# Linear attention with a gated feed-forward layer on one core: a written-out order for all engines, the query decay moved into a cast, even and odd tokens sorted by the store, scores and state alternating, and inter-block products at full size

## The chip, the cores and the metric

One Trainium2 chip, one of its cores. The time is device microseconds of a whole execution, the median of several runs. A profile is one execution seen by the hardware profiler; its span is 1 to 2 us shorter than the time. Engines are named as in the profile: PE is the tensor engine, PEld its weight loads, DVE the vector engine, ACT the scalar engine, POOL GpSimd, SP the engine that issues the transfers (SPq is its queue). Two views are used most. The slices cut the span into 40 equal parts; a digit is the busy share of a part in tenths (9 is 90% or more). The chain of work that ended last starts at the last instruction and goes back, at each step, to whatever released it; a line gives start, length, engine, tile and line of the kernel. GB/s is what all DMA engines together moved.

The profile lists PE's products as 128*128 ("full array") or 64*64 ("64 rows", four quadrants); going from one kind to the other is called a change of its tiling mode here (0.109 us each in the runs below). An eviction is a copy of PE's result out of PSUM. FFN is the feed-forward layer. The turns are products with the identity that bring the result back to rows of tokens.

A ratio of two kernels is the mean time of the fast runs of one over the mean time of the fast runs of the other in the same rounds on the same chip, with a 95% interval. It is therefore not quite the ratio of the medians that are quoted.

## The reference, cut to what matters

```python
# q, k, v: [4, 8, 768, 64]; lam: one decay per head; blocks of 64 tokens
for b in range(nb):
    intra = (qb @ kb.T * Dmask) @ vb               # Dmask[i, j] = lam ** (i - j) for i >= j
    inter = (qb * lam_pow) @ kv_state
    out[b] = intra + inter
    kv_state = lam_block * kv_state + (kb * rev_pow).T @ vb
x = out, tokens x 512                              # 3072 x 512
H = max(x @ w_h, 0);  T = sigmoid(x @ w_t + b_t)
result = T * H + (1 - T) * x
```

Both kernels write the decay as a product: v is scaled by lam^-t and the queries' side by lam^t, so the mask is only a triangle of ones and zeros and the state needs no decay of its own. A step of both is 256 tokens (twelve steps). A partition holds two neighbouring tokens of k, q and v (`(p j)` with j = 0, 1), so a load reads 512 contiguous bytes at a time. After a transpose the 128 tokens of a half stand as "all even ones, then all odd ones". Somewhere they must come back into order; where this happens is one part of the change.

## The kernel before: what the change and the argument touch

The kernel records tasks and a small planner in Python (a model of engine times) sorts them into one static order.

```python
def evac_q(n, p, hs, eng):                   # here even and odd tokens come back into order
    dst = get("qT", n)[:, hs.start // 2:hs.stop // 2].rearrange("p n (q j) -> p n q j", j=J)
    src = get("qtr", n, p).rearrange("p n j q -> p n q j")
    A.activation(dst, src, AF.Copy) if eng == "ACT" else V.tensor_copy(dst, src)

def inter(n):                                # 64-row products, one per head
    ...
    T.matmul(get("o", n)[half(e), b, hp, :], lhsT=get("ss", n, b)[half(e), hp, :],
             rhs=get("qT", n)[half(e), hp, b * C:(b + 1) * C], ...)

def decay(n, b):                             # lam^t, after the attention, on DVE
    V.tensor_tensor(get("xT", g)[:, :, r * C:(r + 1) * C], in0=get("o", n)[:, b],
                    in1=pow_q[:, :, c * C:(c + 1) * C], op=ALU.mult)

def store(n, b, p, js):
    i = (2 * n + b) * C
    nc.sync.dma_start(out=out[i:i + C, js[0] * 128:js[-1] * 128 + 128], in_=get("o_sb", n, b, p))

for t in plan(tasks):
    t.emit()
```

## Time and profile before

| | before |
|---|---|
| time, median of 3 runs | 119.21 us (119.08 to 121.41) |
| span of the profile | 118.0 us, clock granted 1.0 throughout |
| busy: PE, DVE, ACT, POOL | 98.8, 81.1, 70.7, 52.3 us |
| moved by DMA | 27.3 MB, of which 6.29 MB are stores |

The prediction below reads the slices and the chain of waits. One further view of the kernel before is needed for the end of the story: the issues of the store line on the SP queue. The columns of the first line are the number of issues, the time of one issue on SP in ns (minimum, median, maximum) and the first and last start.

```profile
L397 SPq DMA_DIRECT2D out_dram<-o_sb x25: 332/407/1930, 37.3 to 115.2; - x25
...
DMA to landing us min/median/max: 1.9/4.8/6.4
```

A store of 256 KB holds SP for about 0.4 us and has landed 4.8 us later. In the profile no engine waits for one, except at the very end of the program (1.4 us).

### The profile page before, as it was taken

How to read it: one execution, taken by the hardware profiler on the slowest of the kernel's cores; microseconds unless marked ns; L12 is line 12 of the kernel's file. 1: busy time of each engine (PE TensorE's matmuls, PEld its weight loads, DVE VectorE, ACT ScalarE, POOL GpSimd, SP SyncE). 2: the span in 40 equal slices, each digit the busy share in tenths (PEclk: the TensorE clock that was granted, in tenths of full speed). 3: DMA queues.
4: the chain of work that ended last, by engine and by line, in shares of the span. 5: the costliest groups of instructions: out<-in, count | busy, mean ns of one | idle time of the engine just before them, and what ended most of it. 6: DMA issues, size and time to landing. Idle time of an engine off the chain costs nothing.

```text
span 118.0 us, 4685 instructions
## 1 busy us (share of the span) xinstructions
PE 98.8 (84%) x2049; PEld 83.0 (70%) x2049; DVE 81.1 (69%) x138; ACT 70.7 (60%) x135; POOL 52.3 (44%) x52
## 2 busy tenths in 40 slices
PE   0056548776899999999999999999988999999970
PEld 0044436565688878888888888888777888888950
DVE  0539461229768887969869788698698775988460
ACT  3599203393874665784677757837576578353860
POOL 7148432777585765864484647458360000000000
PEclk9999999999999999999999999999999999999999
DMA  0999999899999999999999999999912204004045
GB/s 17 267 304 380 366 294 284 234 252 305 289 293 272 301 290 290 305 300 322 335 290 315 304 265 300 300 315 263 314 64 89 94 0 173 10 6 178 6 178 177
DMA packets 42413, 27.57 MB, mean 234 GB/s; under 512 B 1301, under 2 KB 38425, under 8 KB 42393
## 3 DMA queue, kind: packets, MB, share of 16 engines
q1 hardware_dynamic: 42240, 27.27, 82.4%
q8 instruction: 16, 0.26, 1.0%
q14 instruction: 5, 0.03, 0.1%
q10 hardware_dynamic: 152, 0.01, 0.1%
HBM read 20.98 MB, written 6.29 MB: 231 GB/s over the span
## 4 chain that ended last, share of the span: by engine, by line
PE 67%; DMA 12%; DVE 7%; SPq 4%; issue 3%; ACT 2%; POOL 1%; DVEq 0%
PE w L367 33%; PE w L385 9%; DMA qf<-in_q_dram 8%; PE w L299 8%; PE s L317 6%; PE o L341 5%; DMA w_f<-in_moe_w_h_dram 4%; DVE th L379 4%; SPq L282 4%; PE kv L349 3%; PE o L330 3%; DVE m L321 2%; ACT L376 1%; POOL qb L286 1%; ACT t_sb L376 1%
## 5 line engine op out<-in xcount | busy, mean ns | idle before, releaser
L367 PE MATMUL w<-xT,w_b 128*128 128x256 bf16 (+1 forms) x416 | 49.0, 268 | 0.0
L367 PEld LDWEIGHTS <-w_b 128*128 128x128 bf16 x416 | 36.9, 99 | 4.6
L321 DVE TENSOR_TENSOR m<-s,tri 128x512 bf16<-128x512 f32 x48 | 31.6, 684 | 4.0 <-PE s L317 3.5
L376 ACT ACTIVATE t_sb<-w,bt_col 128x256 bf16<-128x256 f32 (+1 forms) x52 | 21.0, 458 | 18.6 <-PE w L367 17.1
L292 POOL TENSOR_TENSOR vs<-vf,pow_k 128x1024 bf16<-128x1024 f32 (+1 forms) x13 | 23.1, 1778 | 11.7 <-DMA vf<-in_v_dram 9.1
L355 DVE TENSOR_TENSOR xT<-o,pow_q 128x512 bf16<-128x512 f32 x24 | 15.4, 685 | 11.4 <-PE o L341 11.4
L371 DVE SCALAR_TENSOR_TENSOR hmx<-w,xT 128x512 bf16<-128x512 f32 (+1 forms) x26 | 16.7, 642 | 5.5 <-PE w L367 5.4
L286 POOL CAST qb<-qf 128x1024 bf16<-128x1024 f32 (+1 forms) x13 | 12.7, 979 | 16.4 <-DMA qf<-in_q_dram 13.9
L379 DVE TENSOR_TENSOR th<-t_sb,hmx 128x512 bf16<-128x512 bf16 (+1 forms) x26 | 15.8, 606 | 4.7 <-ACT t_sb L376 4.5
L391 ACT ACTIVATE o_sb<-w 128x512 f32<-128x512 f32 (+1 forms) x24 | 13.7, 588 | 7.3 <-PE w L385 7.3
L303 ACT ACTIVATE kT<-w 128x1024 bf16<-128x1024 bf16 (+1 forms) x13 | 12.4, 954 | 6.5 <-PE w L299 6.5
L308 ACT ACTIVATE qT<-w 128x1024 bf16<-128x1024 bf16 x11 | 11.3, 1024 | 7.4 <-PE w L299 7.4
L286 POOL CAST kb<-kf 128x1024 bf16<-128x1024 f32 x11 | 11.9, 1079 | 5.3 <-DMA kf<-in_k_dram 5.3
L385 PE MATMUL w<-id,th 128*128 128x128 bf16 x96 | 13.1, 219 | 0.6 <-DVE th L379 0.6
L385 PE MATMUL w<-id,xT 128*128 128x128 bf16 x96 | 13.2, 220 | 0.0
L317 PE MATMUL s<-qT,kT 64*64 64x128 bf16 x384 | 11.5, 229 | 1.5 <-DVE m L321 1.4
L349 PE MATMUL kv<-vs,kb 64*64 64x64 bf16 x320 | 9.2, 198 | 2.1 <-POOL vs L292 1.4
L349 PEld LDWEIGHTS <-kb 64*64 64x64 bf16 x320 | 7.6, 113 | 4.2 <-issue 4.2
L299 PE MATMUL w<-id,kb 128*128 128x128 bf16 x96 | 8.4, 235 | 2.5 <-POOL kb L286 1.9
L317 PEld LDWEIGHTS <-kT 64*64 64x64 bf16 x384 | 7.5, 110 | 3.9 <-DVE m L321 2.4
L385 PEld LDWEIGHTS <-th 128*128 128x128 bf16 x96 | 9.3, 98 | 1.1 <-DVE th L379 1.0
L385 PEld LDWEIGHTS <-xT 128*128 128x128 bf16 x96 | 9.1, 98 | 1.0
(37 smaller groups left out, 78.3 us busy)
## 6 DMA issues: line engine op xcount, KB each, us to landing
out_dram<-o_sb SPq DMA_DIRECT2D x23, 256.0 KB, 4.8
kf<-in_k_dram SPq DMA_DIRECT2D x11, 512.0 KB, 7.3
qf<-in_q_dram SPq DMA_DIRECT2D x11, 512.0 KB, 7.8
vf<-in_v_dram SPq DMA_DIRECT2D x11, 512.0 KB, 7.1
w_f<-in_moe_w_h_dram SPq DMA_DIRECT2D x4, 256.0 KB, 5.2
w_f<-in_moe_w_t_dram SPq DMA_DIRECT2D x4, 256.0 KB, 5.6
kf<-in_k_dram SPq DMA_DIRECT2D x2, 256.0 KB, 4.7
qf<-in_q_dram SPq DMA_DIRECT2D x2, 256.0 KB, 5.5
```

The costliest lines, as they stand in the source:

```text
L286: eng.tensor_copy(get(x + "b", n)[:, :, hs, :].rearrange("p j h d -> p h j d"), get(x + "f", n, p).rearrange("p h (j d) -> p h j d", j=J))
L292: eng.tensor_tensor(get("vs", n)[:, hs].rearrange("p h j d -> p (h j) d"), in0=get("vf", n, p).rearrange("p h (j d) -> p (h j) d", j=J), i ...
L299: T.transpose(get(x + "tr", n, p)[:, i, j, :], get(x + "b", n)[:, j, h:h + 2, :], id128)
L317: T.matmul(get("s", n, u)[half(b), e, i, j, :], lhsT=get("kT", n)[half(e), hp, j, half(b)], rhs=get("qT", n)[half(e), hp, b * C:(b + 1) * ...
L321: V.tensor_tensor(get("m", n, u)[:, e], in0=get("s", n, u)[:, e], in1=tri[:, None].to_broadcast([128, 2, J, C]), op=ALU.mult)
L349: T.matmul(get("kv", n // NST)[half(e), hp, :], lhsT=get("kb", n)[half(b), j, 2 * hp + e, :], rhs=get("vs", n)[half(b), 2 * hp + e, j, :], ...
L355: V.tensor_tensor(get("xT", g)[:, :, r * C:(r + 1) * C], in0=get("o", n)[:, b], in1=pow_q[:, :, c * C:(c + 1) * C], op=ALU.mult)
L367: T.matmul(get(x, g, js[0])[:, i, :], lhsT=w[:, kc, j * 128:(j + 1) * 128], rhs=get("xT", g)[:, kc, :], start=(kc == 0), stop=(kc == KC - 1))
L371: V.scalar_tensor_tensor(get("hmx", g, js[0]), in0=get("h", g, js[0]), scalar=0.0, in1=get("xT", g)[:, js[0]:js[-1] + 1, :], op0=ALU.max, ...
L376: A.activation(get("t_sb", g, js[0])[:, i, :], get("t", g, js[0])[:, i, :], AF.Sigmoid, bias=bt_col[:, j:j + 1])
L379: V.tensor_tensor(get("th", g)[:, js[0]:js[-1] + 1, :], in0=get("t_sb", g, js[0]), in1=get("hmx", g, js[0]), op=ALU.mult)
L385: T.matmul(get("x", n, b, p)[:, (j - js[0]) * 128:(j - js[0] + 1) * 128], lhsT=get(x, g)[:, j, r * C:(r + 1) * C], rhs=id128, start=(j == ...
```

## The change

Its intent: take the planner's order out and write down one order for all engines, found elsewhere, with a better start; take work off the vector engine; and make tensor-engine work cheaper by fewer changes of its tiling mode. The core of the diff (the order itself, some forty lines of tokens such as `TQ.0.0=0`, is cut):

```diff
-class Task: ...
-def plan(tasks): ...
+PLAN = """
+Lq.0.0 Lq.0.1 Lq.1.0 Lk.0.1 Lv.0.1 Lk.0.0 Lv.0.0 Lk.1.0 CQ.0.1@POOL Lq.1.1 Lv.1.1 ...
+"""
 # query decay: in the cast of q on POOL, no longer after the attention
-    eng.tensor_copy(get(x + "b", n)..., get(x + "f", n, p)...)
+def cast_q(n, p, eng):
+    scale(n, p, eng, "qf", new(("qb", n), ...)..., pow_q)
-    V.tensor_tensor(get("xT", g)..., in0=get("o", n)[:, b], in1=pow_q[...], op=ALU.mult)
+    copy(eng, new(("xT", *g), ...)[:, :, r * C:(r + 1) * C], get("o", n, b))       # DVE or ACT
 # even and odd tokens: no longer sorted at the eviction of q, but by the store
-    dst = get("qT", n)[...].rearrange("p n (q j) -> p n q j", j=J)
-    src = get("qtr", n, p).rearrange("p n j q -> p n q j")
+    copy(eng, new(("qT", n), [128, NP, J, C])[...], get("qtr", n, p))
-    nc.sync.dma_start(out=out[i:i + C, ...], in_=get("o_sb", n, b, p))
+    nc.sync.dma_start(out=out[i:i + C, cs].rearrange("(q j) d -> j q d", j=J), in_=get("o_sb", n, b, p))
 # scores and state alternate
+    for i, (hp, j, x) in enumerate(...):
+        score(n, e, hp, j, x)
+        if st:
+            state(n, b, *st[i])
 # inter: the state is kept as a 128 x 128 block diagonal, one full product for two heads
-    T.matmul(get("o", n)[half(e), b, hp, :], lhsT=get("ss", n, b)[half(e), hp, :], rhs=get("qT", n)[half(e), ...], ...)
+    T.matmul(get("o", n, b)[:, hp, :], lhsT=get("ss", n, b)[:, hp, :], rhs=get("qT", n)[:, hp, :, half(b)], ...)
 # the sigmoid stays in PSUM; its table is loaded ahead
+    A.preload_act_table(AF.Sigmoid)
```

## The prediction

> **What bounds the kernel now.** I read the slices of the page first, because they show whether one limit holds for the whole span.
>
> ```profile
> PE   0056548776899999999999999999988999999970
> PEclk9999999999999999999999999999999999999999
> DMA  0999999899999999999999999999912204004045
> ```
>
> A digit is a slice of 2.95 us. TensorE (PE) is filled from slice 11 (about 33 us) to slice 38, and only partly before that; the DMA engines are full from 3 to 88 us. So there are three stages: a start, in which TensorE waits, a middle, in which it does not, and a tail. The chain of work that ended last, in order of time, names what holds each. First the start:
>
> ```profile
> 6.13 5.03 DMA w_f<-in_moe_w_h_dram
> 11.18 9.08 DMA qf<-in_q_dram
> 20.31 1.05 POOL qb L286
> 21.41 1.05 PE w L299 x8
> 23.52 1.28 ACT L376
> 25.68 1.29 DVE th L379
> 26.98 1.21 DVE m L321 x2
> 28.23 0.42 PE s L317 x16
> ```
>
> Until 20 us the chain is loads: both weight matrices (2 MB) are fetched ahead of the second block's k, q and v, and the second q lands at 20.26. Then come one-time costs in a row: a table load on ScalarE (ACT), a product on VectorE (DVE), two masks. One whole period of the middle, in the same view:
>
> ```profile
> 67.54 0.57 PE o L341 x32
> 68.11 0.30 PE kv L349 x16
> 68.41 1.85 PE w L367 x16
> ...
> 70.86 0.45 PE o L330 x15
> 71.30 0.55 PE w L299 x8
> 71.85 0.87 PE w L367 x8
> 72.73 0.45 PE w L385 x8
> 73.17 0.35 PE s L317 x16
> 73.52 0.55 PE w L385 x8
> 74.07 0.45 PE w L299 x8
> 74.52 0.87 PE w L367 x8
> 75.39 0.57 PE o L341 x32
> ```
>
> No link belongs to another engine: the pieces add up to the period, 75.39 - 67.54 = 7.85 us for a block of 256 tokens. Periods without a second state update take 7.55. Twelve blocks (8 x 7.85 + 4 x 7.55) are 93 us of TensorE issue time. From 33 us to its last matmul at 114.4 TensorE loses about 2.5 us (waits near 39.7, 86.3 and 113.2 to 114.0), so 79 us of the work lie there and 14 before 33 us: **19 us are lost in the start, 2.5 in the middle, 3.6 in the tail** (114.4 to 118.0: last eviction and store).
>
> [...]
> - [...]eight transposes take 0.45 us after other full-array work and 0.55 after 64-row work (67.54 period), and sixteen scores 0.42 against 0.35.
> - [...]the mask, 512 elements from PSUM, takes 684 ns; the gate product on bf16 in SBUF has a median of 415. No contiguous bf16 copy from PSUM on VectorE is in it.
> - [...]The gate product's longest, 1.72 us against the median of 415 ns[...].
> [...]
>
> **The change part by part.** The instruction orders of both builds give the counts.
>
> **Order of the start.** Before, the weights are loads 7 to 14 of the queue. Now fifteen half loads (256 KB) of blocks 0 to 2 come ahead, and the weights follow in four transfers of 512 KB spread between loads of blocks 2 and 3. In the trace before, 256 KB land every 0.75 us from 5.6 us (first k) to 15.4 (last weights), and every 0.86 later. Applied to the new order: blocks 0 and 1 complete at about 13.9 us (before: 22.0), the first half of w_h at 17.9, the second at 20.5, those of w_t at 24 and 26.5, block 3 at about 31. The casts on POOL then pace the start. The decay in the q cast makes it a product like v's, 1.91 us against 1.05 a block. POOL does q0, half of k0 and v0 from about 6.7 us, q1, k1, v1 by 16.5, q2 by 18.4, and v3 at about 33. What TensorE can finish by 33 us is therefore: attention of blocks 0 to 2 (transposes 3.0, scores and state 3.5, inter and intra 2.9), the FFN of blocks 0 and 1 (eight groups of eight matmuls at 0.9: 7.2), one such group of block 2 (0.9), block 3's transposes (1.0), the four turns of blocks 0 and 1 (2.0): 20 us, against 14. **Gain: about 5.5 us.** The sigmoid table is also loaded ahead of time (1.28 us off the chain above), which is inside this figure.
>
> **Inter as full products.** 160 matmuls of 64 rows (0.45 us a block) become 80 of 128x128; at the 0.055 us of a transpose or turn, eight take 0.45. No gain by itself, but inter leaves the 64-row mode. With the new grouping the mode changes fall from 68 to 42 in the built orders. At 0.07 to 0.10 us each, 26 fewer are **2.2 us**. The state eviction doubles in width, 382 to about 597 ns (as the output eviction of 512), 20 times.
>
> **Scores and state alternating.** Sixteen scores take 0.35 and sixteen states 0.24 to 0.30 apart; together 0.59 where they touch. Thirty-two intra products in all four quadrants take 0.57. Alternated scores and states keep four quadrants busy too, so I expect 0.57 a pair. [...] Sum: 0 (within 1 us).
>
> **Query decay in the POOL cast.** The decay product on VectorE (24 x 685 ns) becomes a plain copy of the same length, which ScalarE can take: 13 do. POOL rises by 13 x some 0.85 = 10 us, to about 62; its 4.9 us a block lie under the 7.6 of TensorE after the start.
>
> **Even-odd to the store.** The permuted q eviction becomes contiguous. The relu product takes 682 ns for 512 elements and 424 for 256, so 1.01 ns an element and 0.165 us fixed[...]. ScalarE stays at 1.02. The store's rows keep their length. The sigmoid now stays in PSUM, so the gate product costs 684 ns flat: its mean was 663 with the long ones. Nothing.
>
> **VectorE and ScalarE.** VectorE: masks 32.8, relu 16.7, gate 16.7, eleven copies of o 7.5, ten states 6.8, kT and qT 7.2, the rest 5: 93 us of durations (before 81). Back to back two take 1.28, not 1.37, so some 87 in effect. ScalarE about 71, as before.
>
> **Tail.** Behind the last blocks stand 12 turn matmuls that don't need the last gate; before, TensorE waited 0.9 us there. I take 0.5 us, as a 256 KB store now precedes the last one closely.
>
> **Sum.** TensorE: 93 - 2.2 = 91 us of work; 20 done at 33 us, 71 left, 2 us of waits: last matmul at 106. Tail 3.5: span 109.5. The time is 1.2 us above the span (119.21 against 118.0): **110.7 us**.
>
> **The rivals.**
> 1. *VectorE becomes the bound.* 69 of its 91 us follow after 33 us, against 71 of TensorE: for it speaks that a fixed order leaves it almost no room, against it that overlap makes 69 into 65. Waits of 3 to 5 us: 114 to 116 us.
> 2. *POOL or the loads hold the start.* Every cast is one block late if the DMA is irregular, as it was before (the second k at 17.1, the second q only at 20.3, where 0.86 a load would give 18.4). For it: v3 on POOL at 33 us is just in time. Then the start gives 2 us, not 5.5: 114 us.
> 3. *The start is hidden better than I count, or alternation lets scores hide states* (0.45 a pair: 2 us less on TensorE): 107 to 108 us.
> 4. *Only the order of the start matters and TensorE's work is unchanged*, if the mode change costs nothing: 113 us.
>
> **Range and chances.** Rivals 1 and 2 each have perhaps one chance in four and cost 3 to 5 us, rival 3 one in four and gives 3. So 107.5 to 115.0 us. Faster by over 2% (below 116.8) needs only half of the start's gain: 0.93. Within 2%: 0.05. Slower: 0.02; it would take a wait in every block.
>
> **What would show it.** The PE row of the slices should be filled from slice 8 to 10 on; the second v's cast on POOL should end by 17 us; the first FFN matmul should start near 19 us. In the middle the chain should still be TensorE alone, with a mean period near 7.4 us a block, full-array groups of eight at 0.45 more often than 0.55, alternated pairs near 0.57, eight inter products 0.45. VectorE near 93 us busy, POOL near 62, ScalarE near 71. I am wrong if VectorE links fill the chain after 33 us (rival 1), if "DMA" or POOL ends TensorE's waits up to 40 us (rival 2), or if a period is longer than 7.7 us.

## The result, and the profile after

| | before | after |
|---|---|---|
| time, median of 4 runs | 119.14 us (118.24 to 121.41) | **197.79 us** (197.68 to 198.47) |
| ratio | | 1.665 (1.655 to 1.675) |
| span of the profile | 118.0 us | 196.0 us, mean clock 0.79 |
| busy: PE, DVE, ACT, POOL | 98.8, 81.1, 70.7, 52.3 us | 102.5, 84.3, 64.8, 60.9 us |

The result is correct, and it is slower by two thirds. The prediction was 110.7 us with a range up to 115. No compute engine is busy for over 9 us more than before; yet 78 us of span have been added. The slices of the changed kernel (one digit is 4.9 us) show where, with the bandwidth of the DMA engines in the last row:

```profile
PE   0268999999999060696097096999800000000000
...
PEclk9999999999999855599669859999985555555555
DMA  4999999999663147933455211111111111111110
GB/s 118 297 290 317 322 302 282 294 294 285 198 188 97 52 146 206 264 128 111 142 161 172 96 53 54 55 51 54 51 51 51 52 51 51 51 51 51 50 51 33
```

Three things are to be seen. PE is filled from slice 4 to slice 12 (20 to 64 us, counted from 0), earlier than before, as predicted. Then it has holes; the DMA row has thinned out before that, from slice 10 on (49 us). And from slice 29 on nothing computes; the DMA engines go on at 51 GB/s with a busy share of one tenth, where they moved about 300 GB/s at nine tenths. Stretches of the same profile (length, busy time of PE, PEld, DVE, ACT, POOL with the number of instructions, granted clock, DMA share, GB/s):

```profile
33.00:56.00 23.00, 23.00 (x531) 20.38 (x528) 20.65 (x34) 15.41 (x27) 18.18 (x12) 1.00 0.99 265
56.00:70.00 14.00, 7.46 (x130) 6.33 (x132) 8.07 (x14) 4.53 (x10) 4.79 (x3) 0.89 0.35 109
70.00:102.00 32.00, 18.54 (x296) 15.75 (x292) 11.58 (x19) 9.76 (x16) 9.59 (x6) 0.68 0.54 164
...
142.00:196.00 54.00, 0.00 (x0) 0.00 (x0) 0.00 (x0) 0.00 (x0) 0.00 (x0) 0.53 0.13 49
```

From 33 to 56 us PE is busy without a gap (23.00 of 23.00). The first store is issued at 47 us; the transfers thin out from 49 us on, and PE runs dry at about 64 us. In the last 54 us only stores move: 49 GB/s at a share of 0.13 of 16 engines. **0.13 is about 2/16: as if two of the sixteen DMA engines carried the stores, at about 25 GB/s each.** No view names a single engine, so this is a reading that the experiments have to test. The clock is lower (0.68, 0.53) in the stretches in which PE is partly or wholly idle; in the last 54 us nothing computes, so there it costs nothing. The issues of the store line, in the columns explained above:

```profile
L337 SPq DMA_DIRECT2D out_dram<-o x23: 625/3602/7202, 47.2 to 176.4; - x23
```

The SP queue of the same profile in order of time (start, length, what):

```profile
58.39 4.81 SPq L337 DMA_DIRECT2D out_dram<-o  x2
63.30 4.45 SPq L173 DMA_DIRECT2D qf<-in_q_dram  x1
...
110.56 60.66 SPq L337 DMA_DIRECT2D out_dram<-o  x13
```

An issue of a store now takes 3.6 us in the median, not 0.4, and the issue of the load queued behind two of them takes 4.45. The chain of work that ended last (start, length) says the same: the tensor engine waits for a cast of q, the cast for a load, and the load lands 8.9 us after its issue (qb is the cast q, qf and kf the loads).

```profile
56.94 8.88 DMA qf<-in_q_dram
...
66.05 1.90 POOL qb L191
...
102.26 8.93 DMA kf<-in_k_dram
```

The built programs tell what differs in the store. The listing of the SP instructions (not a profile) has 128 contiguous rows before and a pattern with 2 in front after:

```
before:  L397 DMACopy out_dram<-o_sb    128x512
after:   L337 DMACopy out_0_dram<-o     2x64x512
```

### The profile page after: what moved, and what is told of

It is laid out like the page before. It is cut to its first block, busy times and chain, and to the rows that moved or that the text cites. A ratio compares the mean times of both kernels' runs of the same rounds, so it can differ in the third digit from the quotient of the medians.

```text
span 196.0 us, 4558 instructions
## 1 busy us (share of the span) xinstructions
PE 102.5 (52%) x1969; PEld 88.5 (45%) x1969; DVE 84.3 (43%) x144; ACT 64.8 (33%) x120; POOL 60.9 (31%) x51
## 3 DMA queue, kind: packets, MB, share of 16 engines
HBM read 20.98 MB, written 6.29 MB: 139 GB/s over the span
## 4 chain that ended last, share of the span: by engine, by line
SPq 26%; PE 23%; DMA 13%; issue 5%; POOL 3%; DVE 1%; ACT 1%; POOLq 0%; DVEq 0%; ACTq 0%
SPq L173 21%; PE bt L300 7%; PE bh L300 5%; DMA kf<-in_k_dram 5%; DMA qf<-in_q_dram 5%; DMA w_f<-in_moe_w_t_dram 4%; PE bx L327 3%; SPq L337 3%; PE bs L217 2%; SPq L178 2%; POOL vs L191 2%; PE bo L282 2%; PE bo L272 1%; PE bqtr L205 1%; POOL qb L191 1%
## 5 line engine op out<-in xcount | busy, mean ns | idle before, releaser
L256 DVE TENSOR_TENSOR m<-bs,tri 128x512 bf16<-128x512 f32 x48 | 31.1, 681 | 6.1 <-PE bs L217 5.8
L300 PE MATMUL bh<-xT,w_b 128*128 128x256 bf16 (+1 forms) x208 | 27.6, 284 | 0.3 <-DVE w_b L105 0.2
L191 POOL TENSOR_TENSOR qb<-qf,pow_q 128x1024 bf16<-128x1024 f32 (+1 forms) x13 | 22.9, 1769 | 15.1 <-DMA qf<-in_q_dram 11.4
L191 POOL TENSOR_TENSOR vs<-vf,pow_v 128x1024 bf16<-128x1024 f32 (+1 forms) x12 | 21.9, 1833 | 12.8 <-DMA vf<-in_v_dram 12.8
L300 PE MATMUL bt<-xT,w_b 128*128 128x256 bf16 (+1 forms) x208 | 24.9, 270 | 0.4 <-POOL w_b L105 0.4
L305 DVE SCALAR_TENSOR_TENSOR hm<-bh,xT 128x512 bf16<-128x512 f32 (+1 forms) x26 | 16.3, 642 | 20.3 <-PE bh L300 20.3
L314 ACT ACTIVATE bt<-bt,bt_col 128x256 f32<-128x256 f32 (+1 forms) x52 | 21.9, 431 | 8.9 <-PE bt L300 7.9
L318 DVE TENSOR_TENSOR th<-bt,hm 128x512 bf16<-128x512 f32 (+1 forms) x26 | 16.6, 644 | 2.9 <-ACT bt L314 2.2
L217 PE MATMUL bs<-qT,kT 64*64 64x128 bf16 x384 | 16.0, 233 | 0.3 <-DVE qT L105 0.3
L327 PE MATMUL bx<-id,th 128*128 128x128 bf16 x96 | 14.1, 231 | 0.3 <-DVE th L318 0.3
```

The lines of the kernel that those rows point to most:

```text
L191: ENG[eng].tensor_tensor(dst, in0=get(src, n)[:, heads(p)].rearrange("p h (j d) -> p h j d", j=J), in1=pw[:, n % NST, heads(p), :, None].t ...
L217: T.matmul(get("s", n, e, hp // 2)[half(b), hp % 2, j, :], lhsT=get("kT", n)[half(e), hp, j, half(b)], rhs=get("qT", n)[half(e), hp, :, ha ...
L256: V.tensor_tensor(new(("m", n, e, u), [128, 2, J, C]), in0=get("s", n, e, u), in1=tri[:, None].to_broadcast([128, 2, J, C]), op=ALU.mult)
L300: T.matmul(t[:, r, :], lhsT=w_b[w][:, kc, (2 * u + r) * 128:(2 * u + r + 1) * 128], rhs=get("xT", *g)[:, kc, :], start=(kc == 0), stop=(kc ...
L305: V.scalar_tensor_tensor(new(("hm", g, u), [128, 2, z * C], tag=f"hm{z}"), in0=get("h", g, u), scalar=0.0, in1=get("xT", *g)[:, 2 * u:2 * ...
L314: A.activation(dst[:, r, :], src[:, r, :], AF.Sigmoid, bias=bt_col[:, 2 * u + r:2 * u + r + 1])
```

## The experiments

The theory after this reading, **leading dimension**: a transfer is spread over the DMA engines by its outermost dimension; with 2 there, two engines carry it. Loads would be spread over all 16, so that a load is complete only when its sixteenths on those two engines are through, behind the stores; this last part is argued, as no view follows one load over the engines. So far the theory rests on the share of 0.13 of 16 engines alone.

Rivals: **stride** (rows 4 KB apart in memory are slow to write) and **order of the queue** (the written-out order puts stores between loads, which holds the loads back).

### Two stores in place of one

```diff
-        nc.sync.dma_start(out=out[i:i + C, cs].rearrange("(q j) d -> j q d", j=J), in_=get("o_sb", n, b, p))
+        for j in range(J):
+            nc.sync.dma_start(out=out[i:i + C, cs].rearrange("(q j) d -> j q d", j=J)[j], in_=get("o_sb", n, b, p)[half(j)])
```

> The changed kernel, but each store is issued as two, one for the even and one for the odd rows (64 rows of 2 KB each, same rows at the same places, result right). Theory 'leading dimension': the 2 x 64 x 512 form of the store is carried by 2 of the 16 DMA engines (51 GB/s and a DMA share of 0.13 in its last 54 us); with 64 rows in front all 16 work, the tail of 54 us and the load waits between 56 and 120 us go, and the time is near the 110.7 us predicted (107 to 115). Rival 'stride': rows 4 KB apart in memory are what is slow; then it stays above 180 us. Rival 'order of the queue': stores between loads in the SyncE queue hold the loads back; then the waits from 56 to 120 us stay and the time is above 135 us.

Measured: 118.61 us, ratio to before 0.9935 (0.986 to 1.001), correct. (The experiments were run in several calls; each ratio is against runs of the kernel before in the same rounds, so ratios of different calls can be compared, and medians only roughly.) The same rows go to the same places, 4 KB apart, in the same order of the queue, and 79 us are gone. That removes stride and order of the queue as causes of the loss. It is not the 107 to 115 us that the theory expected, though; the missing microseconds (6.4 against the next run) are followed up below.

### The plain store, rows in wrong order

```diff
-        nc.sync.dma_start(out=out[i:i + C, cs].rearrange("(q j) d -> j q d", j=J), in_=get("o_sb", n, b, p))
+        nc.sync.dma_start(out=out[i:i + C, cs], in_=get("o_sb", n, b, p))
```

> The changed kernel with the plain contiguous store of before (128 rows in order; the even and odd tokens land in wrong rows on purpose). Leading dimension: like the run with two stores, 107 to 115 us, perhaps 1 us less for half the number of stores. Stride: also fast, so this run alone does not tell the two apart. Order of the queue: above 135 us.

Measured: 112.18 us, ratio 0.9403 (0.934 to 0.947); wrong. Everything else in the change is as it was, so everything else together gains 6%. It also lies within the range that was predicted for the whole.

### The kernel before, with only the form of its store changed

```diff
-        nc.sync.dma_start(out=out[i:i + C, ...], in_=get("o_sb", n, b, p))
+        nc.sync.dma_start(out=out[i:i + C, ...].rearrange("(q j) d -> j q d", j=2), in_=get("o_sb", n, b, p))
```

> The kernel before, with only its store written in the 2 x 64 x 512 form (rows wrong on purpose). Leading dimension: stores at 51 GB/s carried by 2 engines, which also carry 2/16 of 21 MB of loads: 6.29 + 2.62 MB at 51 GB/s = 174 us of their time, so 180 to 205 us, with a DMA share of 0.13 at the end. Order of the queue (a fault of the written-out order): stays near 119 us.

> The kernel before with its store in a 4 x 32 x 512 form (rows wrong on purpose, rows 8 KB apart). Leading dimension: 4 engines, 102 GB/s and a share of 0.25 where stores run alone; 6.29 + 5.24 MB at 102 GB/s = 113 us of their time, so 120 to 135 us. Stride: at least as slow as the 2 x 64 form, 180 us or more.

Measured (rows wrong): 199.27 us with 2 in front, ratio 1.673 (1.659 to 1.687), and 144.5 us with 4 in front (two runs, 142.25 and 146.78, the profiled one slow, so no ratio is given). The slices' last rows, first with 2, then with 4:

```profile
DMA  4999999944754442754472472441111111111110
GB/s 103 311 377 293 256 281 292 263 127 140 197 156 142 151 138 61 223 137 147 142 207 71 144 200 79 147 139 48 55 55 51 55 51 51 51 51 51 51 50 33
```

```profile
DMA  1999999999976776666776577667652222222220
GB/s 45 295 348 375 293 265 281 286 285 277 273 217 200 196 196 212 181 179 208 206 200 180 162 208 211 184 200 210 198 148 96 101 94 98 85 101 88 100 94 27
```

Where only stores are left, 2 in front moves about 51 GB/s, 4 in front 85 to 101 GB/s: nearly twice as much with twice the dimension, at about twice the share (0.13 from 144 to 198 us; 0.27 from 107 to 137 us). The kernel before has another order, another decay and other products, and one line brings it to the time of the changed kernel. So the store alone is enough, and the theory agrees with these runs. The time with 4 was expected at 120 to 135 us and came out longer; my sum took the engines' data time only and no waits.

### The rows in order again, twice

If the sorting is not the store's business, it can be done where the attention result is copied out of PSUM (a copy of fp32: on DVE 683 ns for 512 elements, as long as a contiguous bf16 copy takes for 1024, 680 ns), or, as before, at the eviction of q.

```diff
 def take(n, b, eng):
-    copy(eng, new(("xT", *g), ...)[:, :, r * C:(r + 1) * C], get("o", n, b))
+    copy(eng, new(("xT", *g), ...)[:, :, r * C:(r + 1) * C].rearrange("p n (q j) -> p n q j", j=J),
+         get("o", n, b).rearrange("p n (j q) -> p n q j", j=J))
```

> The changed kernel, with the even and odd tokens put back into order where the attention result is copied out of PSUM (one copy per 128 tokens, same number of elements), and the plain contiguous store. Result right. Theory: the order of the rows costs nothing there[...]; so it is the 112.2 us of the run with the plain store in wrong order (111 to 113.5), 0.94 of the kernel before. Rival: a stepped read of PSUM is slow; then the 24 copies take over 750 ns (now about 600 to 684) and the time is above 114 us.

Measured: **112.05 us, ratio 0.9356 (0.929 to 0.943), correct.** The copies take 683 ns on DVE and 595 on ACT, as the contiguous ones of the run with the plain store do (683 and 595). Three of its six runs are slow; the three fast ones average 111.4 us, and the ratio uses these alone.

The other place, with the even-odd part undone alone (permuted eviction of q, triangle in plain order, plain store):

> The changed kernel with the even-odd part alone undone: q is put into order when it is evicted after the transpose, as in the kernel before, and the store is the plain one. Result right. Theory (the 2 x 64 x 512 store is the whole loss, the rest of the change gains what was predicted): 111 to 114 us; the q evictions on VectorE[...] 2 of 1024 elements go from about 0.7 to 1.2 us, 2 of 512 to 0.69, together 1.5 us of VectorE, at most 1 us of the time. Rival (the written-out order needs something else of the even-odd part): above 116 us.

Measured: 112.07 us, ratio 0.9347 (0.929 to 0.941), correct. Both versions beat both kernels, by the same amount. So the even-odd part of the change is worth nothing that these runs can see; moving it to the store cost 86 us. The permuted eviction is not free in itself: in the kernel before, which has it too, 512 bf16 elements take 692 ns on DVE, against 408 contiguous in the version with the order in the copy. But only four evictions of q are on DVE (two of 1024 elements, two of 512), and on ACT 1024 elements take 1024 ns permuted and 1027 contiguous.

The version with the order in the copy is the one that the prediction should be held against. Its slices (2.75 us each):

```profile
PE   0006399799999999999999999996999999999970
...
DMA  1799999999999999999999899999972522020485
```

Its chain of work that ended last, around 90 us:

```profile
90.08 0.57 PE bo L282 x32
...
91.09 2.73 PE bt L301 x24
93.82 1.75 PE bh L301 x16
95.57 0.45 PE bx L328 x8
96.01 0.45 PE bo L272 x8
```

Two of its stretches, in the columns explained above:

```profile
33.00:105.00 72.00, 70.94 (x1533) 63.55 (x1531) 62.76 (x105) 48.21 (x92) 40.43 (x26) 1.00 0.80 240
105.00:110.20 5.20, 1.63 (x27) 1.28 (x23) 1.88 (x5) 1.70 (x5) 0.00 (x0) 0.83 0.68 249
```

PE is filled from slice 5 (14 us) with few gaps, idle for 1.1 of the 72 us from 33 to 105 us, and the links around 90 us are PE's own (bt and bh are products of the FFN, bx turns). Eight inter products (`bo L272`) take 0.45. The links cut out between 90.65 and 91.09 are alternating scores and states; with the intra products (`bo L282`) ahead of them they take 1.01 us.

### Alternating scores and state

```diff
             score(n, e, hp, j, x)
-            if st:
-                state(n, b, *st[i])
+        for s in st:
+            state(n, b, *s)
```

> As the run before in this call, but in each pair first the 16 scores, then the 16 states, not alternating. By the prediction alternation is worth 0 within 1 us (0.57 for a pair, 0.59 apart): within 1 us of the run with the order in the copy. Rival: alternation hides the states under the scores; then this costs 20 pairs x 0.15 = 3 us.

Measured: 111.97 us, ratio to before 0.9418 (0.937 to 0.947) against 0.9356 (0.929 to 0.943) with alternation, in the same rounds. The intervals overlap. The medians are 0.1 us apart, but that with alternation contains three slow runs; the fast runs average 111.4 us with (three) and 112.1 us without (six). In the chain, a pair between two full-array groups takes 0.57 us with alternation (67.21 to 67.78 us) and 0.63 without (37.05 to 37.68 us): at most 20 x 0.06 = 1.2 us. So alternation is worth between nothing and about 1 us, and not 3.

### What a change of tiling mode costs

```diff
         for r in range(2):
+            if r == 1:      # 64x64 (or, in the control, 128 x 64: full array); overwritten by the next group
+                T.matmul(t[0:64, 1, 0:64], lhsT=id128[0:64, 0:64], rhs=id128[0:64, 0:64], start=True, stop=True, ...)
             for kc in range(KC):
```

> As the run with the order in the copy, with one 64x64 product (64 columns, its result overwritten) put into the middle of each of the 52 groups of eight FFN products: 104 more changes between full-array and 64-row work. By the prediction each costs 0.07 to 0.10 us, so 7 to 10 us more than without, against 52 x about 0.03 = 1.5 us for the product itself. Rival (mode changes are free): 1 to 2 us more, like its control.

> Control of the run with mode changes: the product put into the middle of each group is a full-array one (128 rows, 64 columns), so there are no more mode changes. Both theories: 52 x 0.03 to 0.06 = 1.5 to 3 us more than the run with the order in the copy.

Measured: 125.12 us with the small product, 113.81 us with the full one (its profiled run is slow; the medians are of four runs each, and the fast runs alone give the same difference), against 112.05 without either. The 104 extra changes of mode (two in each of 52 groups) cost 125.12 - 113.81 = 11.3 us, **0.109 us each**. In the chain, first with the changes of mode, then in the control:

```profile
90.89 0.44 PE bh L303 x4
91.33 0.14 PE bh L301
91.47 0.98 PE bh L303 x8
```

```profile
84.25 0.44 PE bh L303 x4
84.69 0.03 PE bh L301
84.72 0.87 PE bh L303 x8
```

The product itself costs 0.03 us; going into the other mode adds 0.11 to it and coming back adds 0.11 to the next eight (0.98 for 0.87).

### Why two stores of 64 rows took 118.6 us

Two reasons could be told apart: the number of transfers (25 more, each with its issue on SP), and the rows a transfer covers (64 in place of 128).

```diff
-        nc.sync.dma_start(out=out[i:i + C, cs], in_=get("o_sb", n, b, p))
+        for j in range(2):                                   # two times 64 contiguous rows
+            nc.sync.dma_start(out=out[i + 64 * j:i + 64 * j + 64, cs], in_=get("o_sb", n, b, p)[half(j)])
```

> The kernel with the order put right in the copy (112.05 us), but each store of 128 contiguous rows is issued as two of 64 contiguous rows. Asks why the even and odd rows in two stores took 118.6 us and not 112. Theory 'number of issues': 25 more transfers cost SyncE about 0.6 us each, which delays the loads queued behind them and the last stores: 116 to 119 us. Rival 'stride of the rows': contiguous halves are as fast as one store, 111.5 to 113.5 us.

```diff
+        for x in range(2):                                   # two times 128 rows, half the columns
+            nc.sync.dma_start(out=out[i:i + C, <half x of cs>], in_=get("o_sb", n, b, p)[:, <half x>])
```

> The kernel with the order put right in the copy (112.05 us), each store issued as two of all 128 rows and half of the columns (1 KB a row). As many transfers of the same size as in the runs with two stores of 64 rows (118.6 and 119.1 us), whose tail moved only about 200 GB/s against 327 with whole stores. Theory [...]a transfer of 64 rows is slow whatever their number; here all 128 partitions take part, so 112 to 114 us and about 300 GB/s in the tail. Rival 'number of issues': 118 to 120 us, as with rows.

Measured: 119.13 us, ratio 0.9921 (0.986 to 0.998), with halves of rows; 116.33 us, ratio 0.9774 (0.972 to 0.983), with halves of columns; one store: 0.9356. So neither expectation holds alone. **Two stores of half the columns cost about 4% (0.9774 against 0.9356), the halves of rows another 1.5%.** The first of these is not cleanly the number of transfers: half the columns also means rows of 1 KB and not 2, and no run separates the two. The stride of the even and odd rows plays no part: contiguous halves are as slow as those (0.9921 and 0.9935). The store line on SP, in the columns explained above, of whole stores, of halves of rows and of halves of columns:

```profile
L338 SPq DMA_DIRECT2D out_dram<-o x23: 332/432/1335, 47.4 to 106.9; - x23
```

```profile
L339 SPq DMA_DIRECT2D out_dram<-o x46: 466/596/1494, 47.2 to 113.7; - x46
```

```profile
L340 SPq DMA_DIRECT2D out_dram<-o x46: 332/442/1372, 47.8 to 111.7; - x46
```

The busiest 2 us near the end, of the same three in the same order (the last two figures are the DMA share and GB/s; the profiled run with halves of columns is slow, at 117.07 us):

```profile
107.00:109.00 2.00, 0.00 (x0) 0.00 (x0) 0.42 (x1) 0.00 (x0) 0.00 (x0) 0.86 0.92 327
```

```profile
108.00:110.00 2.00, 1.68 (x31) 1.50 (x28) 1.70 (x4) 1.84 (x5) 0.00 (x0) 1.00 0.90 208
```

```profile
108.00:110.00 2.00, 1.68 (x30) 1.45 (x26) 1.62 (x4) 1.84 (x5) 0.00 (x0) 1.00 0.81 268
```

Halves of rows keep the engines about as busy (0.90 for 0.92) and move 208 GB/s for 327; no view here shows why. Their issue takes 0.60 us for 0.43. Halves of columns have the short issue but twice as many of them. The time goes in two places. From 60 to 80 us PE is busy for 18.96 us with whole stores, 17.17 with halves of rows and 16.29 with halves of columns; over the whole stretch from 33 to 106 us it is idle for 1.1, 3.8 and 3.9 us, and the chain there runs through loads issued between the stores on SP. And the time from the last eviction's end to the end of the span grows from 2.8 to 7.1 and 4.6 us. So both versions lose about 2.8 us in the middle, 4.3 and 1.8 us at the end: what the halves of rows cost on top lies in the tail, where only stores move.

### Does the cast of q pace the start?

```diff
-        scale(n, p, eng, "qf", ..., pow_q)
+        copy(eng, <qb>, <qf>)                # no decay: values wrong on purpose
```

> The kernel with the order put right in the copy (112.05 us), but POOL casts q without the decay (values wrong on purpose), 1.05 instead of 1.91 us a block. Prediction: POOL paces the start, so the block-3 cast of q, which ended TensorE's largest wait there, comes earlier: 0.5 to 2 us less. Rival: the loads pace the start and POOL only waits for them: no difference within 0.5 us.

Measured: 111.55 us, ratio 0.9281 (0.922 to 0.935), against 0.9356 (0.929 to 0.943): 0.5 us in the medians, 0.9 by the ratios of fast runs, intervals overlapping, so inconclusive as a time. The order of POOL's work is clearer. First with the decay, then without (start, length, what, and the idle time before it with its releaser):

```profile
31.49 1.90 POOL L191 TENSOR_TENSOR qb<-qf,pow_q 128x1024 bf16<-128x1024 f32 x1 [0.63 <-PE bt L301]
33.35 1.90 POOL L191 TENSOR_TENSOR vs<-vf,pow_v 128x1024 bf16<-128x1024 f32 x1
```

```profile
31.49 1.04 POOL L105 CAST qb<-qf 128x1024 bf16<-128x1024 f32 x1 [0.61 <-DMA qf<-in_q_dram]
33.31 1.90 POOL L191 TENSOR_TENSOR vs<-vf,pow_v 128x1024 bf16<-128x1024 f32 x1 [0.78 <-DMA vf<-in_v_dram]
```

With a cast half as long v of block 3 starts at the same time, because it has only just been loaded. So at 33 us the loads set the pace, and with the decay POOL just keeps up with them.

### What could not be tried

Two variants were built and not run. Inter as products of 64 rows in the new order would have undone that part alone; the check before the run refused it. The saving in changes of mode is therefore measured only by adding changes, not by undoing the part. And an even-odd store in one transfer with 64 in front was rejected by the check too; so no run has the sorting store in one transfer with more than 2 in front.

## Why the prediction was wrong, point by point

**The step that failed** is the one on the store: "The store's rows keep their length" and, at the end of that part, "Nothing". The length of a row was indeed kept. What changed was the outermost dimension of the transfer, from 128 to 2, and with it, as the theory reads the shares of 0.13 with 2 in front and 0.27 with 4, the number of DMA engines from 16 to 2. The built order that the prediction quotes its counts from had `2x64x512` in it; I read it for counts and not for shape. None of the rivals had it either: one of them treats transfers, but only loads at the start; a slower result was given a chance of 0.02. What showed it: 51 GB/s at a share of 0.13 where only stores move, 144.5 us for 199.3 with 4 in front for 2, and 112 us with the whole change and a plain store. The missing term can be estimated from what the profile shows (2/16 of the loads on the two engines is the theory's part of it): stores of 6.29 MB at 51 GB/s are 123 us of the two engines; by 49 us the slices have moved some 13.7 MB, so about 7.5 MB of loads were still to come, 2/16 of which are 0.9 MB and 18 us. From the first store at 47 us that makes 47 + 123 + 18 = 188 us of the 196. In order of time: computing ends at 142 us and not at 107, as in the versions with a plain store (loads behind stores), and stores alone run on from 142 to 196.

**The other steps**, held against the version with the rows put in order in the copy (112.05 us, fast runs 111.4, for 110.7 predicted):

- *Order of the start and fewer mode changes: right in sum, partly by luck.* Predicted gains 5.5 and 2.2 us. At 33 us the kernel before had 80.2 us of PE busy time left (its stretches from 33 us on), this one has 70.94 and 1.63, together 72.6: 7.6 us less. Neither was isolated by a run of its own in the full kernel, but the counts of instructions before 33 us allow an estimate for the start: four FFN groups more (64 products for 32, the prediction counted on 72), 16 scores and 32 intra products more, three products of turns fewer; at the prediction's own costs that is about 4.3 us. The first FFN product runs at 21.9 us and not near 19. The cost of a change of mode was isolated, and is 0.109 us for the 0.07 to 0.10 assumed, so 26 of them are 2.8 us. One term was too large and the other too small. The 0.07 had no good reading behind it: the sixteen scores of 0.42 and those of 0.35 both follow full-array work in the chain before (at 65.25 and 73.17 us).
- *"The casts on POOL then pace the start": only half right.* The first q cast waits for the decay factors until 7.2 us (6.7 without decay), but at 33 us the loads pace it. The time predicted for the cast of block 3's v, about 33 us, was right (33.35), but because its load had only just landed.
- *Scores and state alternating, 0 within 1 us: right.* A pair between full-array groups takes the 0.57 us estimated (next to intra products 0.44, the rest of the 1.01 above), and the time without alternation differs by 1 us at most.
- *Inter as full products, 0.45 for eight: right.*
- *The contiguous q eviction, worth nothing: right.* A contiguous bf16 copy of 1024 elements on DVE takes 687 (k) and 680 ns (q), and the version with the permuted eviction is no slower (ratio 0.9347 against 0.9356).
- *DVE's 93 us of durations:* the page has 84.6 busy, since the records of back-to-back instructions overlap (48 masks of 681 ns are 32.7 us of durations and 31.0 busy); its waits in the middle are short. One of them, near 71.6 to 75.3 us, is in the chain, and PE loses about 1 us there. Rival 1 was not it. ScalarE was put at 71 us and is busy for 64.5; that miss costs no time. (Rival 1 counts with 91 us where the sum above it says 93.)
- *The 1.3 us that remain:* 72.6 us of work were left at 33 us for 71 predicted (+1.6), waits came to 1.4 for 2 (-0.6), the tail after PE's last matmul is 3.2 for 3.5 (-0.3), and time minus span is 1.9 us for 1.2 (+0.7). Together 1.4. Two of these terms come from misreadings of the kernel before. Its stretches show 80.2 us of PE work after 33 us and 1.3 us lost, not 79 and 2.5. And the 1.2 us of time minus span mix a median with the span of another execution: in every run the two differ by 1.6 to 1.9 us.

## What to carry to other kernels

When a transfer's access pattern is rewritten, look at its outermost dimension in the built program, not at the length of its rows: with 2 in front it moved 51 GB/s at a share of 0.13 of the 16 engines here, and the loads behind it in the queue went down with it (two of 256 KB in the chain landed 8.9 us after issue, against 5.5 in the median with the order in the copy and a plain store). A busy share near a multiple of 1/16 (0.13) with a bandwidth to match (51 GB/s), and issues that take microseconds (3.6 in the median), were its signature in the profile. The permutation was free in a copy of fp32 out of PSUM (683 ns either way), and not in a bf16 copy on DVE (692 ns for 408, 512 elements).
